# The slot experts' second layer with 8 stationary columns per expert, in four parts of 128, 112, 80 and 64 columns

## The chip, the cores and the metric

The kernel runs on one core of a Trainium2 chip. A core has TensorE (PE in the profile; PEld is its loading of stationary operands), VectorE (DVE), ScalarE (ACT), GpSimd (POOL) and SyncE (SP), which here issues all transfers to and from HBM; sixteen DMA engines carry them. Engines run side by side and wait for each other through semaphores; each works through its own instructions in order. The metric is the device time of one execution in microseconds.

## What is computed

Three stages follow each other: a gated linear attention over 4 x 8 heads (768 steps, head size 48), a dense mixture of four experts over its 3072 rows of 384 features, and a soft mixture of eight slot experts. The change lies in the last one alone:

```python
logits = x @ phi                                   # 3072 x 32
d = softmax of logits over the 3072 rows
slot_input = (d.T @ x).reshape(8, 4, 384)          # 8 experts, 4 slots each
for e in range(8):
    h = np.maximum(slot_input[e] @ w1[e], 0.0)     # 4 x 1024
    slot_out[e] = h @ w2[e]                        # 4 x 384
c = softmax of logits over the 32 slots
return c @ slot_out.reshape(32, 384)               # 3072 x 384
```

## The kernel before

Attention and the dense mixture run interleaved, in six blocks of 512 rows; `finish` closes the program with the slot experts, once the last block is there. All names below are in `finish`. TensorE gets its instructions there in the order in which the code issues them, and so does every other engine.

The eight experts are handled as two groups g of four. In a group each expert j has one of TensorE's four column groups, so four products run side by side, with results on partitions 32j to 32j+31. The 32 stationary columns are all 32 slots, though only four belong to the expert of the column group.

- `first(g, half)` is the first layer: stationary sT (the slot inputs, 32 columns), moving w1 in pieces of 256 columns. The result, after ReLU, is hs: row 32j + s holds what slot s would give in expert j.
- `turn(g, half)` turns hs around: four transposes per call into a PSUM tile m, and a VectorE instruction that multiplies by a mask `own`, so that only the slots that belong to an expert keep their values, into hT. `turn(0, 0)` and `turn(0, 1)` stand between the last two calls of `first`; the word t in the list below is the other two.
- `second(i)` is the second layer for part i of the 384 output columns, 128 columns each. A call (word s0, s1, s2) does an eighth of a part: eight fp32 products, stationary a 32-column piece of hT, moving 128 columns of w2, summed in the PSUM tile po. Parts use two tiles in turn (acc0, acc1). All parts use the same pieces of w2 (tiles pl, wr, pr, pc), so the first part also waits for their loads.
- `pick_os(i)` (os0, ...) takes po out of PSUM on VectorE, times the slots' softmax sums; `pick(i)` adds up the rows of each slot with a 0/1 matrix and makes three copies of them (so_p); `split_so(i)` rounds them on ScalarE into so, and VectorE puts the rest of the rounding into the middle copy.
- `combine(i, b)` (c0.0 to c2.5) multiplies so by the row softmax cT for 512 rows (PSUM tile f). ScalarE (even b) or VectorE (odd b) copies the result to ot, and SP issues its transfer to the output.

The order of all this is written out by hand in one list, a word for each call:

```python
CLOSING = "s0 t s0 s0 s0 s0 s0 s0 s0 hint os0 s1 pick0 s1 so0 s1 s1 c0.0 c0.1 c0.2 c0.3 c0.4 s1 s1 s1 s1 os1 s2 pick1 s2 so1 s2 s2 c0.5 c1.0 c1.1 c1.2 c1.3 s2 s2 s2 s2 os2 pick2 so2 c1.4 c1.5 c2.0 c2.1 c2.2 c2.3 c2.4 c2.5"
```

The word hint is where the engines load the flag for a branch that is not taken here.

Of the kernel before, what the change touches and what calls it, by code (L numbers as in the profile page):

```python
# [8 lines left out]
F32 = mybir.dt.float32  # L9
# [17 lines left out]
KT = DM // 128  # L27
# [5 lines left out]
BLOCKS = [512] * 6  # L33
# [10 lines left out]
REST = 18  # L44
CLOSING = "s0 t s0 s0 s0 s0 s0 s0 s0 hint os0 s1 pick0 s1 so0 s1 s1 c0.0 c0.1 c0.2 c0.3 c0.4 s1 s1 s1 s1 os1 s2 pick1 s2 so1 s2 s2 c0.5 c1.0 c1.1 c1.2 c1.3 s2 s2 s2 s2 os2 pick2 so2 c1.4 c1.5 c2.0 c2.1 c2.2 c2.3 c2.4 c2.5"
SLACK = 6
# [36 lines left out]

C_ID, C_MASK, C_SELF, C_SEL, C_SEL3, C_OWN, C_END = 0, 128, 192, 320, 352, 448, 704

# [6 lines left out]
def const_array():  # L92
    c = np.zeros((128, C_END), np.float32)
    i = np.arange(128)
    c[i, C_ID + i] = 1.0
    c[:, C_MASK:C_MASK + SUB] = (np.arange(SUB)[None, :] >= i[:, None] % SUB)
    c[:, C_SELF:C_SELF + 128] = (i[None, :] % 32 == i[:, None] % 32)
    c[:, C_SEL:C_SEL + 32] = (np.arange(32)[None, :] == i[:, None] % 32)
    for r in range(3):
        c[:, C_SEL3 + r * 32:C_SEL3 + r * 32 + 32] = c[:, C_SEL:C_SEL + 32]  # L100
    for g in range(2):
        c[:, C_OWN + 128 * g:C_OWN + 128 * g + 128] = (i % 32 // 4 == 4 * g + i // 32)[None, :]
    return c
# [8 lines left out]
class Net:  # L112
# [425 lines left out]
    def finish(self, pieces, out, rest, spare, announce=lambda: None):  # L538

        nc = self.nc  # L540
        nb = len(BLOCKS)
        c = self.c
# [9 lines left out]
        p = self.mtile([1, 128])  # L552
# [42 lines left out]
        def turn(g, half):  # L595

            if half == 0:
                hT[g] = tp.tile([128, 8, 128], F32, name="hT", tag="hT")
            p = self.mtile([128, 4, 128])
            for k in range(4):  # L600
                f = 4 * half + k
                nc.tensor.transpose(p[:, k, :], hs[g][:, 128 * f:128 * f + 128], c[:, C_ID:C_ID + 128])
            own = c[:, C_OWN + 128 * g:C_OWN + 128 * g + 128]
            nc.vector.tensor_tensor(hT[g][:, 4 * half:4 * half + 4, :], p,
                                    own.unsqueeze(1).broadcast_to([128, 4, 128]), op=ALU.mult)

# [14 lines left out]
        def second(i):  # L621
            if i not in state:
                state[i] = self.ps_a.tile([128, 128], F32, name="po", tag="acc%d" % (i % 2))
                done[i] = 0
            g, fp = divmod(done[i], 4)
            done[i] += 1
            w = [pieces(g, 1, fp, j) for j in range(4)]
            for f2 in range(2):
                f = 2 * fp + f2
                c = DM * f2 + 128 * i  # L630
                for j in range(4):
                    nc.tensor.matmul(state[i][32 * j:32 * j + 32, :], hT[g][:, f, 32 * j:32 * j + 32], w[j][:, c:c + 128],  # L632
                                     start=(g == 0 and f == 0), stop=(g == 1 and f == 7), tile_position=(0, 32 * j))

        def pick_os(i):
            os = oss[i] = tp.tile([128, 128], F32, name="os", tag="os")
            nc.vector.tensor_scalar(os, state[i], s1[:, 3:4], None, op0=ALU.mult)

        def pick(i):
            state[i] = self.ps_a.tile([96, 128], F32, name="so_p", tag="acc2")  # L640
            nc.tensor.matmul(state[i], c[:, C_SEL3:C_SEL3 + 96], oss[i], start=True, stop=True)

        def split_so(i):
            d = slice(128 * i, 128 * i + 128)
            nc.scalar.activation(so[:, d], state[i], AF.Copy)
            nc.vector.tensor_tensor(so[32:64, d], state[i][32:64], so[32:64, d].bitcast(F32), op=ALU.subtract)

        def combine(i, b):
            n = int(self.start[b])
            N = BLOCKS[b]  # L650
            dve = b % 2
            ps = (self.ps_m, self.ps_h)[dve].tile([128, N], F32, name="f", tag="mh"[dve])
            nc.tensor.matmul(ps, so[:, 128 * i:128 * i + 128], self.cT[:, n // CH:(n + N) // CH, :], start=True, stop=True)  # L653
            ot = spare()[:, :N]
            if i == KT - 1 and b == len(BLOCKS) - 1:
                nc.scalar.activation(ot[:, :HALF], ps[:, :HALF], AF.Copy)
                nc.vector.tensor_copy(ot[:, HALF:], ps[:, HALF:])
            elif dve:
                nc.vector.tensor_copy(ot, ps)
            else:  # L660
                nc.scalar.activation(ot, ps, AF.Copy)
            nc.sync.dma_start(out[:, NT * i + n:NT * i + n + N], ot)

# [626 lines left out]
def post(y):  # L1290

    out = np.empty((NCH, CH, DM), y.dtype)
    pos = [b * CPB + c for b, c in ORDER]
    out[pos] = y.reshape(128, KT, NCH, CH).transpose(2, 3, 1, 0).reshape(NCH, CH, DM)
    return out.reshape(NT, DM)
# [17 lines left out]
```

## Time and profile before

| | |
|---|---|
| time, three runs | 934.13, 934.44 and 935.5 us, median 934.44 |
| profiled execution, its own time | 933.92 us |
| its span | 932.1 us |
| TensorE busy, share of the span | 910.8 us, 98% |
| VectorE, ScalarE, GpSimd busy | 620.1, 375.0 and 552.8 us |
| written to HBM | 4.77 MB |

The span is what the profiler saw of the core's work; some 1.8 us of the profiled execution's time lie outside it. A share of busy time is an average over stages with different limits: the closing stage, which the change touches, is the last 45 us.

### The profile page before, as it was taken

To read this page: it belongs to the slowest core of one execution; us is meant where nothing else is said; L and a number is where in the kernel's file an instruction comes from. 1 tells how busy PE (TensorE), PEld (TensorE's weight loads), DVE (VectorE), ACT (ScalarE), POOL (GpSimd) and SP (SyncE) were. 2 spreads that over 40 slices of the span, in tenths; PEclk is the share of its full clock that TensorE was granted. 3 is DMA by queue.
4 is the path that set the end of the run, shared out by engine and by line. 5 is a ranking of instruction groups with operands and counts; after the bars stand their busy time and mean duration, and the time that the engine had idled before them with its cause. 6 is when DMAs were issued, how large, how long until landed. Compare 5 with 4: busy or idle time off the path is not lost.

```text
span 932.1 us, 17618 instructions
## 1 busy us (share of the span) xinstructions
PE 910.8 (98%) x6759; PEld 739.4 (79%) x6759; DVE 620.1 (67%) x1338; ACT 375.0 (40%) x636; POOL 552.8 (59%) x550
## 2 busy tenths in 40 slices
PE   6999999999999999999999999999999999999996
PEld 4898887887888887888887888887878878878764
DVE  7868677399777389787399786378866245555333
ACT  4544443434434334434434434344343334333322
POOL 6746768565687564676575676665576565445300
PEclk7999999999999999999999999999999999999998
DMA  8664531531222332222323213422121235454695
GB/s 242 205 198 140 150 130 54 177 113 58 92 82 78 113 96 76 72 92 82 119 77 95 71 47 124 122 77 69 44 89 46 63 121 179 147 180 148 238 361 207
DMA packets 51723, 113.52 MB, mean 122 GB/s; under 512 B 6832, under 2 KB 16176, under 8 KB 51632
## 3 DMA queue, kind: packets, MB, share of 16 engines
q1 hardware_dynamic: 51632, 112.34, 37.1%
q8 instruction: 54, 0.88, 0.4%
q14 instruction: 37, 0.30, 0.1%
HBM read 105.58 MB, written 4.77 MB: 118 GB/s over the span
## 4 chain that ended last, share of the span: by engine, by line
PE 94%; DMA 2%; DVE 1%; POOL 1%; ACT 1%; issue 0%; SPq 0%; ACTq 0%; DVEq 0%
PE acc L333 42%; PE h L288 42%; PE m L1013 2%; PE m L921 1%; PE m L944 1%; PE po L632 1%; PE h L590 1%; DMA pc<-in_w2p 1%; DMA wr<-in_wm 1%; PE m L467 1%; DMA qkf<-in_qkf 1%; PE m L406 0%; POOL x2T L365 0%; PE f L653 0%; PE O L1010 0%
## 5 line engine op out<-in xcount | busy, mean ns | idle before, releaser
L333 PE MATMUL acc<-hh,whi 128*128 128x512 f32 x1104 | 343.0, 392 | 0.3 <-DVE t L364 0.3
L288 PE MATMUL h<-xt,whi 128*128 128x512 f32 x1104 | 343.1, 392 | 0.0
L221 POOL TENSOR_TENSOR wlo<-wr,whi 128x384 fp32r<-128x384 f32 x188 | 191.0, 1037 | 135.8 <-ACT whi L216 130.7
L221 POOL TENSOR_TENSOR wlo<-pc,whi 128x384 fp32r<-128x384 f32 x184 | 188.3, 1045 | 138.8 <-ACT whi L216 138.6
L288 PEld LDWEIGHTS h<-xt,whi 128*128 128x128 f32 x1104 | 205.1, 188 | 46.8 <-ACT qkf L784 1.9
L333 PEld LDWEIGHTS acc<-hh,whi 128*128 128x128 f32 x1104 | 205.2, 188 | 44.4 <-issue 1.1
L288 PE MATMUL h<-xt,wlo 128*128 128x512 f32 x552 | 215.0, 390 | 0.0
L333 PE MATMUL acc<-hh,wlo 128*128 128x512 f32 x552 | 215.0, 389 | 0.0
L301 ACT ACTIVATE hh<-h 128x512 fp32r<-128x512 f32 (+1 forms) x164 | 95.4, 582 | 218.3 <-PE h L288 217.7
L312 DVE SCALAR_TENSOR_TENSOR hh<-h,hh 128x512 fp32r<-128x512 f32 (+1 forms) x164 | 108.3, 660 | 108.4 <-ACT hh L301 107.0
L288 PEld LDWEIGHTS h<-xt,wlo 128*128 128x128 f32 x552 | 103.6, 188 | 21.8
L333 PEld LDWEIGHTS acc<-hh,wlo 128*128 128x128 f32 x552 | 103.6, 188 | 21.7
L216 ACT ACTIVATE whi<-pc 128x768 fp32r<-128x768 f32 x92 | 77.8, 845 | 95.5 <-PE acc L333 89.4
L216 ACT ACTIVATE whi<-wr 128x768 fp32r<-128x768 f32 x94 | 79.5, 846 | 89.9 <-PE acc L333 82.8
L889 DVE STREAM_TRANSPOSE kn<-qkf 32x128 f32<-32x128 f32 x304 | 91.7, 302 | 11.3 <-POOL qkf L811 4.8
L809 DVE RECIPROCAL R<-G 112x128 f32<-112x128 f32 x80 | 74.9, 941 | 0.4
L819 POOL TENSOR_TENSOR W<-qkf,R 64x256 f32<-64x256 f32 x80 | 59.5, 744 | 6.3 <-DVE R L809 3.3
L365 POOL TENSOR_TENSOR x2T<-x2T,t 128x512 f32<-128x512 f32 x30 | 41.1, 1393 | 22.1 <-DVE t L364 21.9
L304 DVE SCALAR_TENSOR_TENSOR t<-h,pb 128x512 f32<-128x512 f32 x32 | 22.1, 692 | 48.0 <-PE h L288 47.7
L305 ACT ACTIVATE hh<-t 128x512 fp32r<-128x512 f32 x32 | 20.2, 632 | 66.5 <-DVE t L304 66.5
L461 DVE STREAM_TRANSPOSE x2n<-x2T 32x384 f32<-32x384 f32 x80 | 45.6, 569 | 1.4
L977 ACT ACTIVATE L<-stc 48x192 f32<-48x192 f32 x88 | 31.6, 359 | 27.6 <-DVE stc L990 21.5
(191 smaller groups left out, 828.8 us busy)
## 6 DMA issues: line engine op xcount, KB each, us to landing
wr<-in_wm SPq DMA_DIRECT2D x102, 384.0 KB, 4.0
qkf<-in_qkf SPq DMA_DIRECT2D x20, 512.0 KB, 4.8
pr<-in_w2p SPq DMA_DIRECT2D x18, 384.0 KB, 7.5
pb<-pT SPq DMA_DIRECT2D x24, 256.0 KB, 4.5
pc<-in_wm SPq DMA_DIRECT2D x16, 384.0 KB, 5.7
pc<-in_w1p SPq DMA_DIRECT2D x16, 384.0 KB, 3.1
pl<-in_w1p SPq DMA_DIRECT2D x16, 384.0 KB, 4.2
qkf<-in_qkf SPq DMA_DIRECT2D x22, 224.0 KB, 3.7
```

The source lines that it names most:

```text
L216: nc.scalar.activation(hi, raw, AF.Copy)
L221: nc.gpsimd.tensor_tensor(lo[:, w], raw[:, w], hi[:, w].bitcast(F32), op=ALU.subtract)
L288: nc.tensor.matmul(ps, wt[:, kt * 128:(kt + 1) * 128], x[:, xi, kt, cols], start=(k == 0), stop=(k == 8))
L301: nc.scalar.activation(hh[:, 0, :], ps, AF.Relu)
L312: nc.vector.scalar_tensor_tensor(hh[:, 1, :], ps, 0.0, hh[:, 0, :].bitcast(F32), op0=ALU.max, op1=ALU.subtract)
L333: nc.tensor.matmul(acc[d][:, cols], wt[:, DM + d * 128:DM + (d + 1) * 128], hh[:, xi, :], start=(ic % run == 0 and k == 0 and not half), s ...
L365: nc.gpsimd.tensor_tensor(x, x, t, op=ALU.add)
L461: nc.vector.transpose(y[u:u + 32, :, :, g:g + 32], x[g:g + 32, :, :, u:u + 32])
L809: nc.vector.reciprocal(st["R"][:, a], st["G"][:, a])
L819: eng.tensor_tensor(st["W"][r, x, s], st["q"][r, s], st["R"][r, s], op=ALU.mult)
L889: self.nc.vector.transpose(to, st["k_all"][32 * g:32 * g + 32, :, 32 * u:32 * u + 32])
L977: nc.scalar.activation(L[s, c, x], stc[s].rearrange("p a e -> p (a e)"), AF.Copy)
```

## The change

The stationary operand of the second layer becomes 8 columns for each expert instead of 32: hT is 128 x 8 x 32 and holds, for each of a group's four experts, 8 columns, of which four are its slots. `turn` makes it with ordinary fp32 products against a 0/1 matrix of 32 columns (a new use of the constants at C_OWN), where transposes stood, and VectorE only copies. Since 8 of each 32 partitions of po are written by products now, `second` fills po with zeros on VectorE before the first product of a part. The division by the softmax sums moves from `pick_os` to `split_so`. The 384 output columns are taken in four parts of 128, 112, 80 and 64 columns, and the list of words has a fourth part; there are 24 combination products and output transfers instead of 18. The output in HBM is laid out with one row per feature, in runs of 2 KB as before.

```diff
-CLOSING = "... s2 s2 s2 s2 os2 pick2 so2 c1.4 c1.5 c2.0 c2.1 c2.2 c2.3 c2.4 c2.5"
+PARTS = ((0, 128), (128, 112), (240, 80), (320, 64))
+CLOSING = "... s2 s2 s2 s2 os2 s3 pick2 s3 so2 s3 s3 c1.4 c1.5 c2.0 c2.1 c2.2 s3 s3 s3 s3 os3 c2.3 c2.4 pick3 so3 c2.5 c3.0 c3.1 c3.2 c3.3 c3.4 c3.5"
...
-                hT[g] = tp.tile([128, 8, 128], F32, name="hT", tag="hT")
-            p = self.mtile([128, 4, 128])
+                hT[g] = tp.tile([128, 8, 32], F32, name="hT", tag="hT")
+            p = self.mtile([128, 4, 32])
             for k in range(4):
                 f = 4 * half + k
-                nc.tensor.transpose(p[:, k, :], hs[g][:, 128 * f:128 * f + 128], c[:, C_ID:C_ID + 128])
-            own = c[:, C_OWN + 128 * g:C_OWN + 128 * g + 128]
-            nc.vector.tensor_tensor(hT[g][:, 4 * half:4 * half + 4, :], p,
-                                    own.unsqueeze(1).broadcast_to([128, 4, 128]), op=ALU.mult)
+                nc.tensor.matmul(p[:, k, :], hs[g][:, 128 * f:128 * f + 128], c[:, C_OWN + 32 * g:C_OWN + 32 * g + 32],
+                                 start=True, stop=True)
+            nc.vector.tensor_copy(hT[g][:, 4 * half:4 * half + 4, :], p)
...
-                state[i] = self.ps_a.tile([128, 128], F32, name="po", tag="acc%d" % (i % 2))
+                state[i] = self.ps_a.tile([128, PARTS[i][1]], F32, name="po", tag="acc%d" % (i % 2))
+                nc.vector.memset(state[i], 0.0)
...
-                    nc.tensor.matmul(state[i][32 * j:32 * j + 32, :], hT[g][:, f, 32 * j:32 * j + 32], w[j][:, c:c + 128],
+                    nc.tensor.matmul(state[i][32 * j:32 * j + 8, :], hT[g][:, f, 8 * j:8 * j + 8],
+                                     w[j][:, c:c + PARTS[i][1]],
...
-            nc.vector.tensor_scalar(os, state[i], s1[:, 3:4], None, op0=ALU.mult)
+            nc.vector.tensor_copy(os, state[i])
...
-            nc.scalar.activation(so[:, d], state[i], AF.Copy)
-            nc.vector.tensor_tensor(so[32:64, d], state[i][32:64], so[32:64, d].bitcast(F32), op=ALU.subtract)
+            nc.scalar.activation(so[:, d], state[i], AF.Copy, scale=s1[0:96, 3:4])
+            nc.vector.scalar_tensor_tensor(so[32:64, d], state[i][32:64], s1[32:64, 3:4], so[32:64, d].bitcast(F32),
+                                           op0=ALU.mult, op1=ALU.subtract)
...
-            nc.sync.dma_start(out[:, NT * i + n:NT * i + n + N], ot)
+            nc.sync.dma_start(out[d0:d0 + D, n:n + N], ot)
```

What this does to the engines' orders is seen at three places; line numbers after the change are 1 to 4 higher. The first is VectorE from the end of part 0 to the os of part 2. Before:

```order
L637 TENSOR_SCALAR os<-po,s_9187 128x128 [waits DVE_49,PE_49]
L646 TENSOR_TENSOR so<-so_p,so 32x128 [waits Activation_49]
L659 COPY ot<-f 128x512 [waits DMAHW3_49,PE_49]
L659 COPY ot<-f 128x512 [waits DMAHW2_49,PE_49]
L637 TENSOR_SCALAR os<-po,s_9187 128x128 [waits PE_49]
L646 TENSOR_TENSOR so<-so_p,so 32x128 [waits Activation_49]
```

After the change:

```order
L639 COPY os<-po 128x128 [waits DVE_49,PE_49]
L624 MEMSET po 128x112
L648 SCALAR_TENSOR_TENSOR so<-so_p,s_9187,so 32x128 [waits Activation_49]
L663 COPY ot<-f 128x512 [waits DMAHW3_49,PE_49]
L663 COPY ot<-f 128x512 [waits DMAHW2_49,PE_49]
L639 COPY os<-po 128x112 [waits DVE_49,PE_49]
L624 MEMSET po 128x80
L648 SCALAR_TENSOR_TENSOR so<-so_p,s_9187,so 32x112 [waits Activation_49]
```

The fill (MEMSET) of a part's po has come in right behind the os of the part before. The second place is TensorE at the end of part 1. Before:

```order
L632 MATMUL po<-pc,hT 32x128 x16
L632 MATMUL po<-pl,hT 32x128 [waits PE_49]
L632 MATMUL po<-wr,hT 32x128
L632 MATMUL po<-pl,hT 32x128
L632 MATMUL po<-wr,hT 32x128
L632 MATMUL po<-pl,hT 32x128
L632 MATMUL po<-wr,hT 32x128
L632 MATMUL po<-pl,hT 32x128
L632 MATMUL po<-wr,hT 32x128
L641 MATMUL so_p<-os,cst 96x128 [waits DVE_49]
```

After the change:

```order
L633 MATMUL po<-pc,hT 8x112 x16
L633 MATMUL po<-pl,hT 8x80 [waits DVE_49,PE_49]
L633 MATMUL po<-wr,hT 8x80
L633 MATMUL po<-pl,hT 8x80
L633 MATMUL po<-wr,hT 8x80
L633 MATMUL po<-pl,hT 8x80
L633 MATMUL po<-wr,hT 8x80
L633 MATMUL po<-pl,hT 8x80
L633 MATMUL po<-wr,hT 8x80
L643 MATMUL so_p<-os,cst 96x112
```

The wait for VectorE has moved from so_p up to the first product of part 2. The third place is TensorE from the last product of the second layer to the end. Before:

```order
L632 MATMUL po<-pc,hT 32x128 x16
L641 MATMUL so_p<-os,cst 96x128 [waits DVE_49]
L653 MATMUL f<-cT,so 128x512 x2
L653 MATMUL f<-cT,so 128x512 [waits DVE_49]
L653 MATMUL f<-cT,so 128x512 x2
L653 MATMUL f<-cT,so 128x512 [waits DVE_49]
L653 MATMUL f<-cT,so 128x512 [waits Activation_49]
L653 MATMUL f<-cT,so 128x512 [waits DVE_49]
```

After the change:

```order
L633 MATMUL po<-pc,hT 8x64 x16
L657 MATMUL f<-cT,so 80x512 [waits DVE_49]
L657 MATMUL f<-cT,so 80x512 [waits Activation_49]
L643 MATMUL so_p<-os,cst 96x64 [waits DVE_49]
L657 MATMUL f<-cT,so 80x512
L657 MATMUL f<-cT,so 64x512 [waits DVE_49]
L657 MATMUL f<-cT,so 64x512 x2
L657 MATMUL f<-cT,so 64x512 [waits DVE_49]
L657 MATMUL f<-cT,so 64x512
L657 MATMUL f<-cT,so 64x512 [waits DVE_49]
```

Behind the last sums there stood eight combination products of 128 output columns; now there are three of 80 and six of 64, and two of them come ahead of so_p.

## Rows read from the trace of the kernel before

**Rows 1.** The page, the chain that ended last, by engine.

```profile
PE 94%; DMA 2%; DVE 1%; POOL 1%; ACT 1%; issue 0%; SPq 0%; ACTq 0%; DVEq 0%
```

**Rows 2.** The chain of waits, closing stage: start us, us, what.

```profile
899.83 7.70 DMA pc<-in_w2p
...
914.56 0.46 PE so_p L641 x2
...
916.93 0.70 DVE ot L659
...
920.13 0.36 DVE os L637
...
920.54 0.47 PE so_p L641 x2
...
921.68 0.52 PE f L653
...
924.15 0.42 DVE ot L657
```

**Rows 3.** DMA, 920.2 to 932.1 us: tenths busy in 40 slices; issues, KB, us to landing.

```profile
DMA  9999970049999999999999998994212200000000
...
out_y<-ot SPq DMA_DIRECT2D x8, 256.0 KB, 4.4
```

**Rows 4.** DMA, issues after 926.05 us: number, KB each, median us to landing.

```profile
out_y<-ot SPq DMA_DIRECT2D x1, 256.0 KB, 4.2
```

**Rows 5.** Line 662, all eighteen output transfers.

```profile
DMA to landing us min/median/max: 2.0/2.9/4.9
```

**Rows 6.** TensorE in order of time, 911.9 to 914 us: start us, us, engine, line, instruction, count.

```profile
913.03 1.06 PE L632 MATMUL po<-pc,hT 128*32 128x128 f32 x32
913.90 0.27 PE L632 MATMUL po<-pl,hT 128*32 128x128 f32 x1
```

**Rows 7.** TensorE in order of time, 899.2 to 900.9 us.

```profile
899.25 1.09 PE L602 MATMUL m<-cst,hs 128*128 128x128 f32 x8
900.28 0.40 PE L590 MATMUL h<-pl,sT 128*32 128x256 f32 x1
...
900.52 0.38 PE L590 MATMUL h<-pl,sT 128*32 128x256 f32 x1
...
900.73 0.38 PE L590 MATMUL h<-pl,sT 128*32 128x256 f32 x1
```

**Rows 8.** TensorE in order of time, 889.15 to 890 us.

```profile
889.21 0.85 PE L569 MATMUL m<-selF,sacc 128*128 128x32 f32 x6 [0.70 <-DVE sacc L482]
889.90 0.31 PE L434 MATMUL m<-cst,EL 128*128 128x128 f32 x1
```

**Rows 9.** TensorE in order of time, 906.6 to 909.3 us; in brackets idle before, releaser.

```profile
906.67 1.52 PE L632 MATMUL po<-pc,hT 128*32 128x128 f32 x32
908.35 0.29 PE L632 MATMUL po<-pl,hT 128*32 128x128 f32 x1 [0.16 <-issue]
...
908.47 0.27 PE L632 MATMUL po<-pl,hT 128*32 128x128 f32 x1
...
908.50 0.27 PE L632 MATMUL po<-wr,hT 128*32 128x128 f32 x1
...
908.92 0.46 PE L641 MATMUL so_p<-os,cst 128*96 128x128 f32 x2
```

**Rows 10.** VectorE in order of time, 902 to 935 us.

```profile
908.23 0.35 DVE L637 TENSOR_SCALAR os<-po,s 128x128 f32<-128x128 f32 x1 [2.80 <-PE po L632]
...
914.15 0.35 DVE L637 TENSOR_SCALAR os<-po,s 128x128 f32<-128x128 f32 x1 [1.33 <-PE po L632]
```

**Rows 11.** VectorE's groups by shape, whole span: busy us, mean ns of one.

```profile
L435 DVE COPY ELn<-m 128x128 f32<-128x128 f32 x2 | 0.6, 288 | 0.6 <-PE m L434 0.6
L140 DVE MEMSET sacc<- 128x385 f32 x1 | 0.4, 379 | 0.1
L139 DVE MEMSET smax<- 128x1 f32 x1 | 0.1, 59 | 0.8 <-PEq L1302 0.8
```

More of the change, by code (lines that the diff above doesn't have):

```diff
@@ L44 @@
 REST = 18
-CLOSING = "s0 t s0 s0 s0 s0 s0 s0 s0 hint os0 s1 pick0 s1 so0 s1 s1 c0.0 c0.1 c0.2 c0.3 c0.4 s1 s1 s1 s1 os1 s2 pick1 s2 so1 s2 s2 c0.5 c1.0 c1.1 c1.2 c1.3 s2 s2 s2 s2 os2 pick2 so2 c1.4 c1.5 c2.0 c2.1 c2.2 c2.3 c2.4 c2.5"
+PARTS = ((0, 128), (128, 112), (240, 80), (320, 64))
+CLOSING = "s0 t s0 s0 s0 s0 s0 s0 s0 hint os0 s1 pick0 s1 so0 s1 s1 c0.0 c0.1 c0.2 c0.3 c0.4 s1 s1 s1 s1 os1 s2 pick1 s2 so1 s2 s2 c0.5 c1.0 c1.1 c1.2 c1.3 s2 s2 s2 s2 os2 s3 pick2 s3 so2 s3 s3 c1.4 c1.5 c2.0 c2.1 c2.2 s3 s3 s3 s3 os3 c2.3 c2.4 pick3 so3 c2.5 c3.0 c3.1 c3.2 c3.3 c3.4 c3.5"
 SLACK = 6
@@ L82 @@
 RESIDENT = [LAG + (i * (NSTEP - LAG)) // RES for i in range(RES)]
-C_ID, C_MASK, C_SELF, C_SEL, C_SEL3, C_OWN, C_END = 0, 128, 192, 320, 352, 448, 704
+C_ID, C_MASK, C_SELF, C_SEL, C_SEL3, C_OWN, C_END = 0, 128, 192, 320, 352, 448, 512
 def weigh(w, f):
@@ L98, in const_array @@
     c[:, C_SEL:C_SEL + 32] = (np.arange(32)[None, :] == i[:, None] % 32)
+    row, slot = i[i % 32 < 8], 16 * (i % 32 // 4) + 4 * (i // 32) + i % 4
     for r in range(3):
-        c[:, C_SEL3 + r * 32:C_SEL3 + r * 32 + 32] = c[:, C_SEL:C_SEL + 32]
-    for g in range(2):
-        c[:, C_OWN + 128 * g:C_OWN + 128 * g + 128] = (i % 32 // 4 == 4 * g + i // 32)[None, :]
+        c[row, C_SEL3 + r * 32 + slot[row]] = 1.0
+    c[32 * (row // 32) + slot[row], C_OWN + 32 * (row % 32 // 4) + 8 * (row // 32) + row % 32] = 1.0
     return c
@@ L629, in second @@
                 f = 2 * fp + f2
-                c = DM * f2 + 128 * i
+                c = DM * f2 + PARTS[i][0]
                 for j in range(4):
-                    nc.tensor.matmul(state[i][32 * j:32 * j + 32, :], hT[g][:, f, 32 * j:32 * j + 32], w[j][:, c:c + 128],
+                    nc.tensor.matmul(state[i][32 * j:32 * j + 8, :], hT[g][:, f, 8 * j:8 * j + 8],
+                                     w[j][:, c:c + PARTS[i][1]],
                                      start=(g == 0 and f == 0), stop=(g == 1 and f == 7), tile_position=(0, 32 * j))
         def pick_os(i):
-            os = oss[i] = tp.tile([128, 128], F32, name="os", tag="os")
-            nc.vector.tensor_scalar(os, state[i], s1[:, 3:4], None, op0=ALU.mult)
+            os = oss[i] = tp.tile([128, PARTS[i][1]], F32, name="os", tag="os")
+            nc.vector.tensor_copy(os, state[i])
         def pick(i):
-            state[i] = self.ps_a.tile([96, 128], F32, name="so_p", tag="acc2")
+            state[i] = self.ps_a.tile([96, PARTS[i][1]], F32, name="so_p", tag="acc2")
             nc.tensor.matmul(state[i], c[:, C_SEL3:C_SEL3 + 96], oss[i], start=True, stop=True)
         def split_so(i):
-            d = slice(128 * i, 128 * i + 128)
-            nc.scalar.activation(so[:, d], state[i], AF.Copy)
-            nc.vector.tensor_tensor(so[32:64, d], state[i][32:64], so[32:64, d].bitcast(F32), op=ALU.subtract)
+            d = slice(PARTS[i][0], sum(PARTS[i]))
+            nc.scalar.activation(so[:, d], state[i], AF.Copy, scale=s1[0:96, 3:4])
+            nc.vector.scalar_tensor_tensor(so[32:64, d], state[i][32:64], s1[32:64, 3:4], so[32:64, d].bitcast(F32),
+                                           op0=ALU.mult, op1=ALU.subtract)
         def combine(i, b):
@@ L650, in combine @@
             N = BLOCKS[b]
+            d0, D = PARTS[i]
             dve = b % 2
[L652 to L655, printed above, removed]
+            ps = (self.ps_m, self.ps_h)[dve].tile([D, N], F32, name="f", tag="mh"[dve])
+            nc.tensor.matmul(ps, so[:, d0:d0 + D], self.cT[:, n // CH:(n + N) // CH, :], start=True, stop=True)
+            ot = spare()[:D, :N]
+            if i == len(PARTS) - 1 and b == len(BLOCKS) - 1:
                 nc.scalar.activation(ot[:, :HALF], ps[:, :HALF], AF.Copy)
@@ L1293, in post @@
     pos = [b * CPB + c for b, c in ORDER]
-    out[pos] = y.reshape(128, KT, NCH, CH).transpose(2, 3, 1, 0).reshape(NCH, CH, DM)
+    out[pos] = y.reshape(DM, NCH, CH).transpose(1, 2, 0)
     return out.reshape(NT, DM)
@@ L1307 @@
         args[name] = nc.dram_tensor(f"in_{name}", a.shape, mybir.dt.from_np(a.dtype), kind="ExternalInput").ap()
-    out = nc.dram_tensor("out_y", (CH, NCH * DM), F32, kind="ExternalOutput").ap()
+    out = nc.dram_tensor("out_y", (DM, NT), F32, kind="ExternalOutput").ap()
     with tile.TileContext(nc) as tc:
```

## Prediction

> **What bounds the kernel now.** I read the page's shares first: the chain that ended last is TensorE for 94% of the span [rows 1]. The change touches only the closing stage, so that stage is read by itself, from the chain of waits over the last 35 us [rows 2]. It shows three different limits in a row. Up to 907.5 the last load of second-layer weights (pc) ends the wait. From there to 920.1 TensorE runs almost without a break: three parts of the second layer (po), each followed by os, so_p, so, and the combination products (f) of the part before. From 920.13 TensorE has nothing left but six products that need the last part, and they wait for os, so_p and so in turn: 1.55 us to the first product (921.68), 2.89 us to the last eviction (924.57). Behind that stands the output traffic: eight of the eighteen output transfers are issued after 920.2, and the DMA engines are full from 922.6 to about 928.4 without a break [rows 3]. The last transfer is issued at 926.1 (a window from 926.05 holds one issue), lands 4.2 us later [rows 4], where the eighteen take 2.0 to 4.9 [rows 5], and the span ends 1.8 us after that. So 11.97 us lie between the last os and the end of the span. The change can shorten that tail; what it does to the 12.6 us ahead of it, and to the stage before, decides.
>
> **What a round of the second layer costs.** A fp32 product of this layer runs as two passes, and four of them, for the four column groups, run side by side. 32 passes, eight such rounds, take 913.90 - 913.03 = 0.87 us [rows 6]: 109 ns for 128 moving columns. The first layer has the same 32 stationary columns and 256 moving ones; its round takes 900.73 - 900.52 = 0.21 us [rows 7]. So the moving columns set a round, 0.85 ns each, and the load of the stationary columns hides. Eight stationary columns instead of 32 then save nothing by themselves, and the four widths give 109, 95, 68 and 54 ns. All widths together are 384 columns as before, so the whole layer costs the same TensorE time.
>
> **Step 1, the turn.** hs is turned by two pairs of turn calls. Before, a pair is eight transposes of one pass: 900.28 - 899.25 = 1.03 us [rows 7]. Now each is a fp32 product with 128 stationary and 32 moving columns, so two passes. The trace has exactly this shape: six passes in 889.90 - 889.21 = 0.69 us, 0.115 each [rows 8]. Sixteen take 1.84 us, 0.81 more a pair, 1.62 us for both. Before, part 0 lost time at its end to the late weight load: its last 32 passes took 1.52 us where the same number took 1.06 in part 1 [rows 6, 9], 0.46 us. That wait is used up first, and +1.16 us is left. Bounds: 0, if the weights still decide; +1.62, if nothing is absorbed. The rows are of the very shapes, so I take +1.16. VectorE's hT copies get smaller (128 columns for 512); nothing waited for them, so this is worth nothing. os0 moves from 908.23 [rows 10] to 909.39.
>
> **Step 2, the cleared sums.** Each po is now filled with zeros by VectorE, and that fill stands behind the os of the part before, on the same engine (the order shown above). The first set of a part, which TensorE used to run while os was being made, must now wait for os and the fill. Prices: a 128x128 copy out of PSUM takes 0.288 us; a fill 0.059 us plus 0.83 ns a column (0.379 for 385 columns) [rows 11], so 0.15, 0.12 and 0.11 for 112, 80 and 64 columns. Copies of 112 and 80 columns I put at 0.27 and 0.25, with a slope like the fill's. The fills in the trace go to SBUF; for PSUM I bound them by 0.06 and by a copy of that width, 0.27, and keep the value. A signal from VectorE to TensorE takes 0.05 (os2 ends at 920.49, so_p begins at 920.54) [rows 2].
> - Parts 0 to 1: TensorE went on 0.12 us after os0 began (908.23, 908.35) [rows 9, 10]; the profile gives no releaser for that gap. Now 0.29 + 0.15 + 0.05 = 0.49: +0.37. Part 1 has 32 rounds, each 14 ns shorter: -0.44. os0 to os1 was 5.92 and becomes 5.85: os1 at 915.24.
> - Parts 1 to 2: part 2 began 0.25 ahead of os1 (913.90, 914.15) [rows 6, 10]. Now it begins 0.27 + 0.12 + 0.05 = 0.44 behind: +0.69. Of this 0.09 was already lost: so_p, which ran 0.57 after the first set began at the earlier boundary (908.35, 908.92) [rows 9], came at 914.56 instead of 914.47 [rows 2]. Net +0.60. Part 2's rounds: 32 x 41 ns = -1.30. os1 to os2 was 5.98 and becomes 5.28: os2 at 920.52.
>
> **Step 3, a fourth part.** Between os2 and os3 stands what stood between os1 and os2: boundary, 32 rounds, one so_p, five products. Taken from 5.98: the boundary +0.57 (with 80- and 64-column prices), 32 rounds of 54 instead of 109 ns -1.76. The fifth product there waited some 0.2 us for VectorE's eviction (the ot at 916.93 stands in the chain) [rows 2]; the new fifth is ScalarE's and doesn't. 4.6 to 4.8, I take 4.7: os3 at 925.2. Thus the last part's sums are complete 5.1 us later than the last part's were before.
>
> **Step 4, the tail.** From os3 on, two products of part 2 come before so_p, and their evictions stand ahead of so on ScalarE and VectorE (about 0.3 more): 1.85 us to the first product of part 3. The six products and evictions have the same 512 columns: 2.89. I give fewer partitions no discount: no eviction of fewer partitions stands in these rows, and a discount would only move the forecast by what is in the range. After os3 nine transfers are left, 3 x 160 and 6 x 128 KB, 1.25 MB instead of 2.1 MB. Before, 2.1 MB needed 5.8 us, 360 GB/s; 128 KB take 0.36, less than the 0.48 at which evictions follow each other (2.89 / 6). So the transfers keep up with the evictions, the last is issued soon after the last eviction: between 0 and the 1.5 that the backlog made of it before (924.57 to 926.1), I take 0.4. Its landing is near the median of the eighteen, 2.9 [rows 5]; the bounds are the shortest, 2.0, and the 4.2 of the last one before. With 1.8 to the end: 1.85 + 2.89 + 0.4 + 2.9 + 1.8 = 9.84, 2.13 us less than 11.97.
>
> **Sum.** 925.2 + 9.84 = 935.04 against 932.1: +2.94 us. The profiled execution took 933.92 us, 1.8 outside its span; it would become 936.86. The median of the runs shown is 934.44, half a microsecond above the profiled one, so on that footing 937.4.
>
> **The other ways.**
> - *The weights still decide (17%).* If the last second-layer weights land so late in the new run that the longer turn fits in front of them, step 1 is free: 937.4 - 1.16 = 936.2. For it: the chain goes through that very load at 907.5. Against: that load was issued at 899.83 [rows 2], before the first word of the closing list, and the wait was only 0.46.
> - *A floor under narrow rounds (7%).* No round narrower than 128 columns stands in this stage. If TensorE could not start its products faster than one in 25 ns, a round of four would take 100: 32 x (5 + 32 + 46) ns = +2.65, 940.0. The four starts of a round lie within 0.03 us here (908.47 to 908.50) [rows 9], which speaks against it, but 109 ns then pass until the next four. The Trainium skill states this floor ("TensorE: Matmul & The Clock Gate", "Wait — 56ns, not 53.3ns?": start to start never under about 25 ns however narrow the product). By that rule parts 2 and 3 would gain nearly nothing from being narrow; the rows agree with it only if it holds for each column group alone.
> - *The loads set the rounds (5%).* 109 ns is also four loads of 32 columns in turn, 27 each. Then 8 columns take 7, and if the moving columns by themselves ran at twice the speed (0.43 ns each), parts 1 to 3 would take 32 x (48 + 34 + 27) ns = 3.5 instead of 6.9 us: 937.4 - 3.4 = 934.0, not slower. It decides once the mean round of these parts falls from 72 ns to about 41, where the 2.94 us are gone. Against it: with the same loads, 256 columns took 0.21 us, twice as long [rows 7].
> - *The rest (9%)*: a tail with landings of 2.0 and cheap fills, 936.2 to 935.5, or something not seen.
>
> **Numbers.** Forecast as summed: 62%. A measurement of this kernel tells about 0.2% (1.9 us) from no change. The forecast and the floor lie beyond it, the late weights right at its edge, the load case inside it. Slower 74%, within 20%, faster 6%. The range reaches from below the late weights (936.2) to the tail with the late landing (938.7) and part of the floor: 935.8 to 939.2.
>
> **What would show it.** In the new profile: the turn's sixteen passes at 1.8 us a pair; no wait for the weight load ahead of os0; TensorE waiting for VectorE's fill at three boundaries, 0.4 to 0.7 us each; rounds of 95, 68 and 54 ns; os3 near 925; the DMA engines with gaps in the last 7 us, and a last landing near 933. I am wrong if the turn runs at 109 ns a product, if the fills do not stand behind os, or if the last landing follows os3 by less than 7 us.

## The result, and the profile after

The changed kernel takes 938.82 us, median of six runs (938.47 to 941.34), against 934.29 us (932.3 to 935.5) before: ratio 1.0054 [1.0044, 1.0064], some 0.5% slower. By the ratio that is 939.3 us for 934.3. The forecast was 937.4 with a range of 935.8 to 939.2: the direction was right, the size too small. The median itself lies inside the range, the time by the ratio just above its upper end.

The profiled execution took 938.8 us, its span 936.9, 4.8 more than before. Not all of that is the change. The product that makes the slot inputs starts ahead of everything that was edited; it came 0.46 us later in this execution than in that of before (889.21, [rows 8]). From there to the end of the span it was 932.1 - 889.21 = 42.9 us and is 47.2: **4.3 us more, where the steps of the prediction summed to 2.94.** The rows of TensorE in order of time answer to [rows 6 to 9]:

```profile
889.67 0.85 PE L570 MATMUL m<-selF,sacc 128*128 128x32 f32 x6 [0.71 <-DVE sacc L483]
...
899.72 1.97 PE L603 MATMUL m<-cst,hs 128*128 128x32 f32 x16
901.62 0.40 PE L591 MATMUL h<-pl,sT 128*32 128x256 f32 x1
...
910.52 0.26 PE L633 MATMUL po<-pl,hT 128*8 128x112 f32 x1 [0.59 <-DVE po L624]
...
914.04 0.95 PE L633 MATMUL po<-pr,hT 128*8 128x112 f32 x32
914.81 0.95 PE L633 MATMUL po<-pc,hT 128*8 128x112 f32 x32
916.39 0.23 PE L633 MATMUL po<-pl,hT 128*8 128x80 f32 x1 [0.63 <-DVE po L624]
...
919.79 0.74 PE L633 MATMUL po<-pr,hT 128*8 128x80 f32 x32
920.35 0.74 PE L633 MATMUL po<-pc,hT 128*8 128x80 f32 x32
921.66 0.22 PE L633 MATMUL po<-pl,hT 128*8 128x64 f32 x1 [0.58 <-DVE po L624]
...
924.46 0.63 PE L633 MATMUL po<-pr,hT 128*8 128x64 f32 x32
924.91 0.63 PE L633 MATMUL po<-pc,hT 128*8 128x64 f32 x32
925.47 0.69 PE L657 MATMUL f<-cT,so 96*80 96x512 f32 x2
...
927.36 1.90 PE L657 MATMUL f<-cT,so 96*64 96x512 f32 x6 [0.81 <-DVE so L648]
```

To read here: the turn of a pair takes 901.62 - 899.72 = 1.90 us (1.03 before); the first product of each later part waits for VectorE's fill, named as releaser, three times 0.6 us; and eight rounds take 914.81 - 914.04 = 0.77, then 0.56 and 0.45 us, 96, 70 and 56 ns each. VectorE in order of time gives the ends of the parts, for [rows 10]:

```profile
910.00 0.29 DVE L639 COPY os<-po 128x128 f32<-128x128 f32 x1 [2.91 <-PE po L633]
910.31 0.15 DVE L624 MEMSET po<- 128x112 f32 x1
...
915.82 0.28 DVE L639 COPY os<-po 128x112 f32<-128x112 f32 x1 [1.09 <-PE po L633]
916.12 0.12 DVE L624 MEMSET po<- 128x80 f32 x1
...
921.15 0.24 DVE L639 COPY os<-po 128x80 f32<-128x80 f32 x1 [0.56 <-PE po L633]
921.41 0.11 DVE L624 MEMSET po<- 128x64 f32 x1
...
925.60 0.22 DVE L639 COPY os<-po 128x64 f32<-128x64 f32 x1 [0.45 <-PE po L633]
...
929.72 0.42 DVE L661 COPY ot<-f 64x256 f32<-64x256 f32 x1 [0.37 <-ACT ot L660]
```

The last part's sums were complete at 925.60, the last copy out of PSUM ended at 929.72 + 0.42 = 930.14, and the span ended only 6.8 us later. The chain of waits for the closing stage, start us, us, what, which answers to [rows 2]:

```profile
901.69 2.73 PE h L591 x48
...
906.76 3.22 PE po L633 x112
...
925.14 3.19 DMA out_y<-ot
...
```

The load of pc is gone from it, as step 1 said. A transfer stands near its end: a copy needed the buffer of ot that this transfer held. By engine, 94% of the chain are TensorE, as in [rows 1]. What fills the 6.8 us is on SyncE's queue and the DMA engines. First SyncE's issues in order of time (the last two rows are narrower windows on the end of the second), then the DMA view of 925.6 to 936.9 us, then of the last 4.6 us (the q1 line: packets, MB, share of 16 engines):

```profile
919.34 2.38 SPq L666 DMA_DIRECT2D out_y<-ot  x5
925.63 7.29 SPq L666 DMA_DIRECT2D out_y<-ot  x11
928.05 4.87 SPq L666 DMA_DIRECT2D out_y<-ot  x7
932.37 0.56 SPq L666 DMA_DIRECT2D out_y<-ot  x1
```

```profile
DMA  8899969999999989888999689689985000000000
GB/s 297 276 326 305 305 218 297 283 276 276 290 283 283 261 254 276 239 225 239 218 239 218 152 218 232 152 196 210 232 174 145 7 0 0 0 0 0 0 0 0
```

```profile
q1 hardware_dynamic: 240, 0.38, 37.3%
...
out_y<-ot SPq DMA_DIRECT2D x1, 128.0 KB, 2.6
```

Eleven transfers are issued, 7.29 / 11 = 0.66 us each on average. Up to 928.05 SyncE keeps pace with the copies: that issue starts right behind the copy that it carries (VectorE, 927.34 + 0.69 = 928.03). Behind it come the six transfers of 64 rows, (932.37 - 928.05) / 6 = 0.72 us apart, while the copies go on at less than 0.5, so that the last issue begins 2.23 us behind the last copy. Five transfers of 112 and 128 rows ahead of them were issued in 2.38 / 5 = 0.48 us each. The engines have work all the time, yet carry less and less: some 300 GB/s at first, 145 to 240 at the end, where the transfers of 64 rows are. Before, the engines were as full [rows 3], at 311 to 379 GB/s in the window that [rows 4] is from.

### The profile page after: what moved, and what is told of

It is laid out like the page before. It is cut to its first block, busy times and chain, and to the rows that moved or that the text cites. A ratio compares the mean times of both kernels' runs of the same rounds, so it can differ in the third digit from the quotient of the medians.

```text
span 936.9 us, 17956 instructions
## 1 busy us (share of the span) xinstructions
PE 914.8 (98%) x6911; PEld 742.2 (79%) x6911; DVE 620.7 (66%) x1347; ACT 377.3 (40%) x640; POOL 552.1 (59%) x550
## 4 chain that ended last, share of the span: by engine, by line
PE 94%; DMA 2%; DVE 1%; POOL 1%; ACT 1%; issue 0%; SPq 0%; ACTq 0%; POOLq 0%; DVEq 0%
PE acc L334 42%; PE h L289 42%; PE m L1017 2%; PE m L925 1%; PE m L948 1%; PE po L633 1%; PE h L591 1%; DMA wr<-in_wm 1%; DMA qkf<-in_qkf 1%; PE m L468 1%; PE m L407 0%; POOL x2T L366 0%; PE m L603 0%; DMA out_y<-ot 0%; PE O L1014 0%
## 5 line engine op out<-in xcount | busy, mean ns | idle before, releaser
L893 DVE STREAM_TRANSPOSE kn<-qkf 32x128 f32<-32x128 f32 x304 | 91.7, 302 | 11.3 <-POOL qkf L815 4.8
```

Source lines behind the costliest of these rows:

```text
L893: self.nc.vector.transpose(to, st["k_all"][32 * g:32 * g + 32, :, 32 * u:32 * u + 32])
```

## The experiments

A new point of measure serves in all of them: the **tail**, from the start of the last os to the end of the span. It was 932.1 - 920.13 = 11.97 before and 936.9 - 925.60 = 11.3 after; the prediction had 9.84. Ratios are to the kernel before, timed on the same chip beside it; each tail is that of one profiled execution. Where a profile alone is compared, the times of the slot-input product and of os are taken from it.

| run | time, us | ratio and interval | tail, us |
|---|---|---|---|
| after | 938.82 | 1.0054 [1.0044, 1.0064] | 11.3 |
| turn of before | 937.67 | 1.0039 [1.0026, 1.0053] | 11.8 |
| fills ahead | 936.91 | 1.0028 [1.0018, 1.0039] | 11.8 |
| alternating halves | 938.82 | 1.0053 [1.0039, 1.0066] | 11.0 |
| merged transfers | 938.26 | 1.0046 [1.0032, 1.0060] | 10.9 |
| spread partitions | 939.14 | 1.0059 [1.0046, 1.0073] | 11.0 |
| spread and merged | 937.49 | 1.0041 [1.0027, 1.0055] | 10.2 |
| doubled issues | 942.11 | 1.0090 [1.0076, 1.0103] | 14.5 |
| pairs in one PSUM tile | 937.20 | 1.0036 [1.0024, 1.0048] | 10.0 |
| pairs by address | 951.04 | 1.0189 [1.0175, 1.0203] | 24.1 |
| four parts alone | 936.68 | 1.0035 [1.0022, 1.0049] | 11.6 |
| four parts, pairs by address | 961.25 | 1.0294 [1.0280, 1.0308] | 36.5 |
| four parts, pairs in PSUM | 934.21 | 1.0003 [0.9994, 1.0012] | 9.3 |
| spread, two queues | 938.53 | 1.0052 [1.0039, 1.0066] | 11.4 |
| before, two queues | 933.95 | 1.0005 [0.9996, 1.0013] | 12.1 |

**Steps 1 and 2, each undone alone.** The turn of before in the changed kernel:

```diff
-                nc.tensor.matmul(p[:, k, :], hs[g][:, 128 * f:128 * f + 128], c[:, C_OWN + 32 * g:C_OWN + 32 * g + 32],
+                nc.tensor.transpose(p[:, k, :], hs[g][:, 128 * f:128 * f + 128], c[:, C_ID:C_ID + 128])
...
-                    nc.tensor.matmul(state[i][32 * j:32 * j + 8, :], hT[g][:, f, 8 * j:8 * j + 8],
+                    nc.tensor.matmul(state[i][32 * j:32 * j + 8, :], hT[g][:, f, 36 * j + 12 * g:36 * j + 12 * g + 8],
```

> The kernel after with the turn of the kernel before: eight one-pass transposes a pair and the masked multiplication, hT 128 wide; of it the second layer takes the 8 columns that hold an expert's slots. Step 1 of the prediction says the turn cost 1.62 us, less 0.46 of weight wait that comes back: the time falls by 1.2 (bounds 0.8 and 1.6) to about 937.6, os0 about 1.2 us earlier. Rival (the last weights decide when part 0 ends): os0 and time stay, 938.6 to 938.8.

Measured: 937.67, where 937.6 was expected. Counted from the slot-input product, os0 came at 908.31 - 889.36 = 18.95 us instead of 910.00 - 889.67 = 20.33. The turn is worth 1.4 us, and the chain of waits of this run has the load of pc again, up to 907.6, the wait that step 1 said the longer turn uses up. The rival, late weights, falls.

The fills ahead:

```diff
         def pick_os(i):
+            if i + 1 < len(PARTS):
+                clear(i + 1)     # tile po of part i + 1 and its memset
```

> The kernel after, with each part's fill of po queued on VectorE ahead of the os of the part before instead of behind it, so that it is done while that part's sums still run. Step 2 of the prediction says that the three boundaries cost 0.4 to 0.7 us each because TensorE waits for os and fill: the gaps of 0.8 us between the parts fall to 0.1 to 0.2, so_p waits for os up to 0.1, os3 comes 1.2 to 1.8 us earlier, and the time falls to 937.0 to 937.6. Rival (the fills hide behind os, and the boundary is os's own wait, or the transfers at the end set the time): less than 0.5 us, 938.4 or more.

Measured: 936.91. VectorE's rows of this run, first part to last:

```profile
909.26 0.29 DVE L645 COPY os<-po 128x128 f32<-128x128 f32 x1 [2.26 <-PE po L637]
913.34 0.12 DVE L623 MEMSET po<- 128x80 f32 x1
914.41 0.28 DVE L645 COPY os<-po 128x112 f32<-128x112 f32 x1 [0.95 <-PE po L637]
...
923.01 0.22 DVE L645 COPY os<-po 128x64 f32<-128x64 f32 x1 [0.45 <-PE po L637]
```

A fill now stands a microsecond ahead of the os that it used to follow, and os0 to os3 takes 13.75 us instead of 15.60: 1.85 less, a little over the top of the expected 1.2 to 1.8. So the place of the fills in VectorE's queue was the price, not the fills. In both runs the tail grew to 11.8 us: half a microsecond is given back there, and the last issue stands 2.8 and 2.5 us behind the last copy, not 2.2. What causes that was not tested.

**Why the tail is longer than forecast.** Four theories. A: 64 rows on one half of the partitions are slow, and alternating halves would help. B: an issue has a price of its own, whatever it carries. C: the new layout in HBM is slow. D: the rate goes by which partitions a single transfer reaches. The first two runs, with their edits:

```diff
+            r = 64 if D == 64 and dve else 0        # alternating halves
-            ot = spare()[:D, :N]
+            ot = spare()[r:r + D, :N]
```

> The kernel after, but the odd blocks of the last part (64 columns) are copied to partitions 64 to 127 of ot instead of 0 to 63; number, size and rows of all transfers stay. Theory A (a transfer over few partitions moves slower per byte, because the transfers of one half of the partitions share the way out of that half): two transfers in flight now use both halves, SyncE's issues in the last part take about 0.4 us instead of 0.55 to 0.9, the last issue ends within 1.2 us of the last eviction instead of 2.8, and the span is 1.0 to 1.8 us shorter, about 937.3 in time. Theory B (every transfer costs its queue some 0.6 us, whatever its rows): issues and time stay as after, 938.8. Theory C (the new order of the output in HBM makes packets slow): as after, too.

```diff
+            elif dve:        # merged: one transfer for two blocks of the last part
+                nc.sync.dma_start(out[d0:d0 + D, n - N:n + N], oss["ot"][:D])
```

> The kernel after, but the six transfers of the last part (64 partitions, 128 KB each) become three of 256 KB, each over two blocks of 512 rows, still over partitions 0 to 63; packets of 4 KB instead of 2. Theory A (few partitions are slow per byte): 384 rows of 2 KB take as long as before, at 200 to 230 GB/s three transfers take 3.4 to 3.9 us, the last landing and the time stay within 0.4 us of after, 938.4 to 939.2. Theory B (a fixed cost of some 0.6 us per transfer): three issues less, 1.5 to 1.8 us shorter, about 937.2. Theory C: packets twice as long in HBM would be faster per byte, some of the same gain.

Neither moved much: the tail fell by 0.3 and by 0.4 us, where A had promised the first 1.0 to 1.8 and B the second 1.5 to 1.8. The merged run's transfers of 4 KB rows still moved at some 230 GB/s from the last copy on, on engines that were busy.

Then the 64 features were put on every second partition, so that neither number, size nor place in HBM of any transfer changed:

```diff
-            nc.sync.dma_start(out[d0:d0 + D, n:n + N], ot)
+            nc.sync.dma_start(out[d0:, n:n + N], whole[0:128:2, :N])      # last part; so has zeros between its columns
```

> The kernel after, but the 64 features of the last part lie on every second of the 128 partitions (so has 64 more columns, the odd ones zero; f and ot of that part have 128 rows, and the transfer reads partitions 0, 2, 4, ... of ot). Number, rows, bytes and places in HBM of all transfers stay. Theory D (the rate of a transfer goes by how many of the ways out of the SBUF its partitions reach, and 64 neighbouring partitions reach half of them; neighbouring transfers run one behind the other on all engines, so that alternating halves gained nothing): the last six transfers take some 0.36 us instead of 0.6, SyncE's issues 0.4, GB/s in the last microseconds above 300, and the time falls by 1.0 to 1.6 us to 937.2 to 937.8. Theory B (a cost per transfer) and theory C (the layout in HBM): as after, 938.8.

The time did not fall. The profiled execution lost 1.7 us ahead of the second layer: its chain has 7.07 us of h from 890.64, that of after 5.39 from 890.88. The granted clock of TensorE was 0.50 there, the lower of its two levels (1.2 GHz), behind the same wait of 0.7 us for sacc after which it stayed at 1.00 in after (start:end and length in us, then busy us of TensorE, its weight loads, VectorE, ScalarE and GpSimd, granted clock, DMA share, GB/s):

```profile
890.90:894.00 3.10, 3.10 (x36) 1.60 (x32) 1.98 (x8) 0.31 (x1) 0.00 (x0) 0.50 1.04 418
```

Whether the other four executions had it too is not known. So the tail is what can be compared: 938.0 - 927.04 = 11.0. The DMA view of its last 4.3 us is another one:

```profile
DMA  9861018997008995300000000000000000000000
GB/s 400 305 229 38 38 38 324 381 343 248 0 0 305 343 362 191 95 0 0 0 0 0 0 0 0 0 0 0 0 0 0 0 0 0 0 0 0 0 0 0
...
q1 hardware_dynamic: 233, 0.37, 23.9%
```

A data packet of 2 KB takes 23.9% x 16 x 4.3 us / (233 - 50 small ones) = 90 ns here, against 37.3% x 16 x 4.6 / (240 - 53) = 147 ns in after, and the transfers are bursts at 300 to 400 GB/s with idle engines between. Fuller engines are not the reason for the 147: in before, from 926.05 on, they were fuller still and a packet from 128 partitions took 41.2% x 16 x 6.05 / (493 - 65) = 93 ns:

```profile
q1 hardware_dynamic: 493, 0.88, 41.2%
```

So D holds for the packets, and the layout in HBM (C), which is the same, is not what made them slow. What is left is the gap between issues: six in 4.21 us. This suggested that two limits lie side by side. The last cell of the table of two by two, and the direct test of an issue's price:

```diff
+                nc.sync.dma_start(out[d0:, n - N:n + N], oss["ot"][0:128:2])      # spread and merged
```

> Both edits of the last part together: the 64 features on every second partition, and one transfer of 64 rows of 4 KB for two blocks; with after, the merged and the spread run this makes a table of two by two, with the same copies out of PSUM in all four. Theory E (two limits lie side by side: 64 neighbouring partitions move 128 KB in some 0.6 us, and an issue on SyncE's queue takes some 0.65 us once several transfers are in flight, so that taking away either leaves the other): the ratio to before falls from 1.0054 to 1.0035 or less, about 2 us below after, with the last landing within 3.6 us of the last copy instead of 4.8. Rival (the end is set by something else, such as the latency of the last landing alone): no further below after than the merged run, ratio 1.0046.

```diff
+            W = HALF if D == 64 else N           # doubled issues
+            for v in range(0, N, W):
+                nc.sync.dma_start(out[d0:d0 + D, n + v:n + v + W], ot[:, v:v + W])
```

> The kernel after, but each of the six transfers of the last part becomes two of 64 rows and 256 columns: twelve issues instead of six, the same bytes over the same partitions. Theory B or E (an issue takes some 0.65 us in a backlog, whatever it carries): six issues more cost 3.3 to 4.0 us, about 942.5, ratio 1.009. Rival (only bytes and partitions count): 938.8 to 939.6, ratio 1.0054 to 1.0063.

SyncE with doubled issues, in order of time, with its DMA view of 932.2 to 936.6 us; then the DMA view of the spread and merged run from its last copy on:

```profile
924.04 12.56 SPq L668 DMA_DIRECT2D out_y<-ot  x19
...
932.18 4.42 SPq L668 DMA_DIRECT2D out_y<-ot  x7
```

```profile
DMA  7960039920169830169720288710379500399300
...
out_y<-ot SPq DMA_DIRECT2D x7, 64.0 KB, 2.0
```

```profile
DMA  9997988699989683412211102000000000000000
GB/s 358 417 417 328 417 328 328 268 417 387 387 328 417 268 298 149 119 60 89 89 60 60 60 30 89 0 0 0 0 0 0 0 0 0 0 0 0 0 0 0
...
out_y<-ot SPq DMA_DIRECT2D x1, 256.0 KB, 4.0
```

The doubled run was slower as expected (ratio 1.0090, tail +3.3): nineteen issues at 0.66 us, though twelve of them carry 64 KB. The last seven still take 4.42 / 7 = 0.63 us each, though the DMA engines stand idle between them, so neither bytes nor packets hold them back. That shows B for transfers of 64 rows: the issue itself sets the pace. With both edits the engines run at 270 to 417 GB/s without gaps, and the tail falls by 1.1 us, where the single edits gave 0.4 and 0.3: more than their sum. The part of the tail from the last copy to the last landing says it more clearly: 4.8 us in after (930.14 to 934.9), 4.8 merged, 4.4 spread, 4.0 with both. What merging alone gained lies behind the last landing, 1.5 us to the end in the two merged runs and 2.0 in the other two; no run says why. The expected 2 us, and a landing within 3.6 us of the last copy, did not come: 256 KB that are issued right after the last copy still take 4.0 us to land, where after had 2.23 + 2.6. In time the gain is 1.0041 against 1.0054, with intervals that overlap; the tails, one execution each, are what carries this point.

**Other versions.** One that takes out both limits and half of the last copies:

```diff
+                nc.tensor.matmul(ps, so[:, base[i] + 64 * (1 - h):base[i] + 64 * (1 - h) + 128], self.cT[:, k:k + N // CH, :],
+                                 start=h == 0, stop=h == 1)      # two blocks into one PSUM tile of 128 rows
```

> The kernel after, but in the last part two products for two blocks go into one PSUM tile of 128 rows: the stationary operand is the 64 columns with 64 zeros behind them for the one and with 64 zeros ahead for the other, summed. So there are three copies of 128x512 and three transfers of 256 KB over 128 partitions instead of six and six, and the output rows of that part lie in HBM in runs of pairs. Theory E: both limits are gone and the copies take 1.5 us less, so the end comes 2.5 to 3.5 us earlier: ratio 1.002 to 1.003. Rival (the landing latency, not the number or the partitions, sets the end): 1.3 to 1.6 us earlier, by the copies alone, ratio 1.0038.

The ratio was 1.0036 and the tail 1.3 us shorter: the size that the rival gave, about half of what theory E promised. The rival's reason does not hold, though: the copies ended only 0.2 us sooner (4.35 us after os3 instead of 4.54), though they were half as many; each now has two products ahead of it. From the last copy to the last landing it was 4.1 us for 4.8. So taking out both limits is worth less than E said.

A pair of blocks as one transfer of 128 partitions, with the two halves as the outer dimension of the address in HBM:

```diff
+                nc.sync.dma_start(out[d0:d0 + D, n - N:n + N].rearrange("d (h n) -> h d n", h=2), oss["ot"][:, :N])
```

> The kernel after, but in the last part the copy of an odd block goes to partitions 64 to 127 of the ot of the even block before it, and one transfer takes both: three transfers of 256 KB over 128 partitions, where the experiment with the merged transfers had three of 256 KB over 64 partitions with longer rows. Theory D (ways out of the SBUF): the three run at some 370 GB/s, 0.7 us each instead of 1.2, and the time is 1.2 to 1.8 us below after, 937.0 to 937.6, and 0.6 to 1.2 below the merged ones. Theory B: the same as the merged ones, 938.3. Theory C: not faster than the merged ones, whose rows in HBM are longer.

> The four parts alone with widths of 128, 128, 64 and 64 columns, and in both parts of 64 columns one transfer of 128 partitions for two blocks, as in the experiment with pairs; turn, 32 stationary columns and no fills as before. Theory D: 935.7 less 1.2 to 1.8 at the end, 933.9 to 934.5, no slower than before (934.3). Theory B or C: 935.2 or more.

Both failed for a reason of their own. The DMA view of the first, from the end of its last issue on:

```profile
GB/s 57 46 80 46 57 40 46 52 52 52 52 52 52 52 52 52 52 52 52 46 57 46 52 52 52 52 52 52 52 52 52 52 52 46 23 29 11 0 0 0
...
q1 hardware_dynamic: 315, 0.63, 11.4%
```

A steady 52 GB/s at 11% of the engines' time is two engines of sixteen. So these two runs tell nothing about partitions. The Trainium skill ("DMA: Bandwidth & Descriptors", "Why a DMA increments its semaphore by 16 and not by 1") says why: the number of engines is the largest, up to 16, that divides the slowest dimension of each of the two address patterns, and that of the pattern in HBM was 2 here.

> The four parts alone: parts, list of words and layout of the output as after; turn, 32 stationary columns, the scaling in os and no fills as before. By the steps of the prediction and the runs so far the turn is worth 1.2 and the fills 1.9 us, so 938.8 - 3.1 = 935.7, some 1.4 us above before. Rival (8 stationary columns save something in the rounds or the loads that 32 columns lose again): 936.5 or more, with rounds above 109, 95, 68 and 54 ns.

Measured 936.68, 1 us above the expected 935.7 and where the rival put it. By its profile os0 to os3 takes 923.00 - 908.75 = 14.25 us, 0.5 more than with 8 columns and fills ahead. One part is so_p, which waits 0.18 and 0.20 us at two boundaries for an os that also multiplies (0.35 us where the copy takes 0.29). The first of them:

```profile
914.60 0.43 PE L643 MATMUL so_p<-os,cst 128*96 128x112 f32 x2 [0.18 <-DVE os L639]
```

Another is the rival's, on a small scale: eight rounds with 32 stationary columns take 0.79, 0.58 and 0.47 us (112, 80 and 64 columns), with 8 columns 0.77, 0.56 and 0.45, so a part of 32 rounds some 0.08 us more. TensorE also waits for the last weights again for 0.16 us, ahead of os0. The extra part is the dearest piece of the change by itself: ratio 1.0035.

> The four parts alone, widths 128, 128, 64 and 64, with the turn, the 32 stationary columns and no fills as before, and in both parts of 64 columns the pairs of blocks in one PSUM tile: eighteen copies and eighteen transfers of 128 partitions as before, and of the last part only three. Theory E: the extra part costs six products of 0.24 us and a so_p of 0.46, 1.9 us; behind the last sums the copies take 1.4 us less and the backlog of transfers (1.5 us ahead of the last issue, and a landing of 4.2 instead of 2.9) goes: 2.9 to 4.2 less. So 1 to 2.3 us faster than before, ratio 0.9975 to 0.999. Rival: what the smaller last part saves is less than the extra products cost, ratio 1.000 to 1.002.

This one ends level with before: the last os came 2.4 us later (922.56 for 920.13) and the tail was 2.7 us shorter. It is the best version with four parts, and no gain; the rival's numbers fit.

**One queue or two.** ScalarE issued the even blocks' transfers of the last part, in the spread run and in the kernel before:

```diff
+                q = nc.sync if dve else nc.scalar
+                q.dma_start(out[d0:, n:n + N], whole[0:128:2, :N])
```

> The run with the last part on every second partition, but the transfers of its even blocks are issued by ScalarE, which copies them, instead of SyncE. An issue takes ScalarE some 0.35 to 0.4 us, so the last copy comes up to 0.8 us later. If the 0.65 us between issues belong to SyncE's queue, it has three issues less behind the copies: the last issue follows the last copy by less than 0.5 us instead of 2.1, and the time falls by 1.0 to 1.4 us, ratio to before 1.0045 to 1.0048 instead of 1.0059. If all issuers share it, ScalarE's own issues take 0.55 us and more as well, the last issue comes no earlier, and the ratio stays at 1.0059 or rises.

> The kernel before, with the transfers of the even blocks of its last part issued by ScalarE. Its last eight transfers of 256 KB kept the engines full from 922.6 to 928.4 us, so the bytes set its end, not the issues: whichever holds, the time stays within 0.8 us of before, ratio 0.999 to 1.001; the last issue comes earlier only if the queue was the limit, and the last landing then takes as much longer.

In the first, an issue kept ScalarE for 0.48 to 0.74 us, not 0.4, so that the last copy came 7.1 us after os3 instead of 4.65; the backlog was gone for that reason, and the run can't tell whether the price of an issue belongs to the queue or is shared. That stays open. In the kernel before, nothing changed, as expected: its last issue stood right behind the last copy and the end stayed where it was. There the bytes decide.

The two runs, and that with pairs in one PSUM tile, do bear on what makes an issue long. How long the issues lasted (ns, shortest, median and longest), 64 rows on ScalarE, 128 rows on ScalarE, 128 rows on SyncE at the end of the pairs' run:

```profile
L674 ACTq DMA_DIRECT2D out_y<-ot x3: 478/574/741, 928.2 to 930.8; - x3
L663 ACTq DMA_DIRECT2D out_y<-ot x3: 338/338/390, 922.0 to 924.2; - x3
L672 SPq DMA_DIRECT2D out_y<-ot x3: 350/383/1083, 928.2 to 929.9; - x3
```

ScalarE had issued nothing ahead of them in either run, and the transfers of 128 rows landed later (up to 5.4 us). So a full queue alone does not make an issue long, and the rows point to the shape of a transfer, 64 rows against 128. No run changed that alone, and one issue in the last row took 1.08 us: the cause stays open.

## Why the prediction was right in direction and too small

- **What a round costs: right.** 109, 95, 68 and 54 ns were forecast; the later three show 96, 70 and 56. Eight stationary columns saved next to nothing, 2 to 3 ns a round. The floor of 25 ns and the loads as rivals fall; the Trainium skill's floor ("TensorE: Matmul & The Clock Gate", "Wait — 56ns, not 53.3ns?") does not hold across column groups here: four passes, one in each group, in 56 ns.
- **Step 1: right.** 1.90 us a pair for 1.84; no load of weights ends a wait ahead of os0; os0 came 1.31 us later, counted from the slot-input product, for 1.16. Undone, 1.4.
- **Step 2: right.** The fills took 0.15, 0.12 and 0.11 us, as put, and TensorE waited for them at all three boundaries. Less the 0.46 us of late start, os1 and os2 came at 915.36 and 920.69; forecast 915.24 and 920.52.
- **Step 3: right, with some luck.** os3 at 925.14 on the same footing, forecast 925.2. From os2 to os3 it was 4.45 us for 4.7, below the stated 4.6 to 4.8, and that made up for what steps 1 and 2 were short of.
- **Step 4: failed.** Forecast 9.84 us, measured 11.3, and this is the whole error of 1.4 us. Its pieces: 4.54 us from os3 to the end of the last copy (4.74 forecast); **2.23 to the last issue (0.4 forecast)**; 2.6 to its landing (2.9); 2.0 to the end (1.8). The sentence that failed is "128 KB take 0.36, less than the 0.48 at which evictions follow each other (2.89 / 6). So the transfers keep up with the evictions". It priced a transfer by bytes alone, at the rate of transfers over 128 partitions, and an issue at nothing. Two things stand against it: an issue of 64 rows keeps SyncE some 0.65 us whether it carries 64 or 128 KB, shown by the doubled issues, and 64 neighbouring partitions move 2 KB rows at 147 ns a packet instead of 90, shown by the spread run. For 128 KB both come to about 0.6 us, so either alone kept most of the tail. With both taken out, the last landing came 4.0 us behind the last copy instead of 4.8; the forecast had 3.3, and the rest of the way stays open. The sign that was named, engines with gaps and a last landing near 933, did not come: the engines were busy, and it landed at 934.9. The step also counted nine transfers behind os3 where there were eleven; that cost nothing, as SyncE still kept pace with the copies at 928.05.

The profile of before could not have given the price of a 64-row issue. SyncE's last eight issues there, in order of time, the first row for all and the others for the last three:

```profile
921.89 5.20 SPq L662 DMA_DIRECT2D out_y<-ot  x8
...
924.38 0.62 SPq L662 DMA_DIRECT2D out_y<-ot  x1
...
925.09 0.93 SPq L662 DMA_DIRECT2D out_y<-ot  x1
...
926.11 0.97 SPq L662 DMA_DIRECT2D out_y<-ot  x1
```

5.20 / 8 = 0.65 us is only an average: the first five took (924.38 - 921.89) / 5 = 0.50 us each, behind copies at 0.48, and the last ones 0.71 and 1.02, while 256 KB took the full engines 0.7. But it showed that an issue has a price, and with it the bound to keep: at 0.65 the six last transfers need 3.9 us, their copies 2.9. The second stands in the Trainium skill ("SBUF — State Buffer", "Door 1: The DMA port swizzle"): partitions 0 to 63 reach half of the ways out of the SBUF, and it gives 196 GB/s for them at 1 MiB. The trace agrees (150 to 240 GB/s at the end of after); I did not weigh it.

The other 0.46 us of the 4.8 is the later start of the closing stage in that execution; the spread of six runs (938.47 to 941.34) covers it.

## What to carry to other kernels

Cutting the last piece of work smaller helps a tail only if its transfers get cheaper with it: count the issues left behind the last sum, times what one takes, beside the bytes. Spreading a small transfer over all partitions was not enough here (no gain in time); two blocks in one tile of 128 rows gave 1.3 us of the tail. When a cleared buffer is new, clear it ahead of the instruction that the next stage waits for, not behind.

## What the runs showed of the hardware that was not expected

- Issues of 64 rows on SyncE take 0.63 to 0.72 us each on average, with 64 or 128 KB alike, and with DMA engines that stand idle between them too; five issues of 112 and 128 rows took 0.48 us each. An issue of 64 rows kept ScalarE for 0.48 to 0.74 us, one of 128 rows for 0.34 to 0.39.
- 64 rows on partitions 0 to 63 are slow, 147 ns a packet of 2 KB, and alternating with 64 to 127 shortened the tail by only 0.3 us; on every second partition a packet takes 90 ns.
- A transfer whose address has 2 as its outermost dimension ran at 52 GB/s, on some two engines of sixteen.
